# Batches 4 to 7 of the first product by seven products, behind all attention; PSUM as eight named banks

## The chip, the core and the metric

The kernel runs on one core of a Trainium2 chip. The metric is device microseconds of one execution. The kernel before takes 393.91 us (median of three runs, 393.77 to 394.09). The engines are named as in the profile: PE is the matrix engine (TensorE), PEld its weight loads, DVE the vector engine, ACT the scalar engine, POOL and SP the two engines that mostly issue transfers here. SBUF is the memory that the engines work from, PSUM the small one that PE writes its products to.

## The reference

Two layers are chained. The first is attention with 8 batches, 12 heads, 448 tokens and 64 numbers per head; the second is a feed-forward pair of products with a SiLU gate between them, 768 to 2048 to 768, over all 3584 tokens. Inputs to the kernel are cast to fp16 in SBUF's tiles.

```python
scores = scale * np.matmul(q, k.transpose(0, 1, 3, 2))
scores = scores - np.max(scores, axis=-1, keepdims=True)
attn = np.exp(scores)
attn = attn / (np.sum(attn, axis=-1, keepdims=True) + 1e-09)
attn_out = np.matmul(attn, v)
x = attn_out.transpose(0, 2, 1, 3).reshape(B * S, H * D)
h = x @ w_in
g = h * (1.0 / (1.0 + np.exp(-h)))
out = g @ w_out
```

## The kernel before

**Attention.** The twelve heads of a batch go in three groups of four; a group of one batch is a unit, and batch 0 is cut into two pieces of tokens, so that there are 27 units. POOL issues the loads of K (tile `rk`), Q (`rq`) and V. DVE turns K and Q (`turn_k`, `turn_q`, L302 and L312). PE makes a burst of scores (`scores`, `scores_rest`, L325): the four heads sit in four groups of 32 rows of the array and run side by side, one head to a bank of PSUM. ACT takes the exponential (`expo`, L362) of two heads at a time, 128 x 896 numbers, into a tile `E`. For most units DVE adds three `E` tiles into `T` (`add_e`, L373) for the sums of the softmax; PE makes the sums (`attend_sums`, L404, or `attend` with part 0, L388) and the two halves of the product with V (`attend`, L388; parts 1 and 2). DVE turns, inverts and turns back the sums (`inverse`, L447, L455, L461) and scales the product into `xT` (`norm`, L477).

**First product.** For batches 0 to 5, `ffn1` (L491) makes one bank of 128 features x 448 tokens in six products (chunks of 128 of the 768 inputs). ACT takes tanh of it into `th` (`tanh`, L502), DVE makes the gated value from `th` and the bank (`gate`, L536) and writes it to `G`, or for some tokens of batches 1 and 5 to `X`. `norm` halves x, so that (1 + tanh) * h is the wanted SiLU.

Batches 6 and 7 are done as a pair by Strassen's scheme in Winograd's form (`pair_product`, L625). The two batches and the two halves of the 768 inputs make a 2 x 2 matrix of blocks, the halves of the inputs and of the 2048 features another. Seven block products of three matrix products each replace eight. For that, DVE makes four sums of x (`combine_x`, L583, tiles `sx`) and four sums of w_in in two halves (`combine_w_in`, L601, tiles `tw`). For each of the eight values of f, the seven products come in the order 1, 6 and 7, 5, 2, 3, 4, and take four banks. Their readers are two copies on ACT (`pair_copy`, L650), five additions on DVE (`pair_add`, L656) and four SiLUs on ACT (`silu`, L663).

**Second product.** Tiles of 128 tokens go in pairs ("quads", fourteen of them). The first quad is a plain product (`plain`, L710); the others go by the same scheme, seven products of eight matrix products with 384 columns (`product`, L696). DVE makes four sums of `G` for each (`combine_g`, L686, tiles `S`) and the additions behind it (`take_6` and its like, L750), ACT two copies (L754, L757). SP stores the results; the last quads' stores are shared with ACT's queue.

**PSUM.** Eight banks: two tiles of two banks (tag `s`) for scores, four tiles of one bank (tag `m`) for everything else. The pair borrows one `s` tile.

**The order.** The order on every engine is fixed when the kernel is built. A class `Order` plays the work through with costs per operation. At each point it chooses for PE among the next burst of scores (not more often than `PACE`), the next attention product and the first of the queue `moe` whose inputs and banks are free; for ACT and DVE it chooses the ready operation with the lowest time plus `bias`. POOL's loads are in one fixed order, each waiting for its buffer. A whole `ffn1` group of six products, or eight for a quad, is one piece of work and isn't interrupted. Until the first `ffn1` group, PE's waits are filled with small products of zeros (L1459). A change of kind on PE, between products that use the whole array and the four-way ones of scores (by rows) or attention (by columns), costs the planner `SWITCH`.

Of the kernel before, what the change touches and what calls it, by code (L numbers as in the profile page):

```python
# [17 lines left out]
PE_OUT = 0.20  # L18
# [11 lines left out]
def act(n):  # L30
    return n * 0.00087 + 0.13


class Ring:


    def __init__(self, n):
        self.free = [0.0] * n

    def can(self, n, now):  # L40
        return len(self.free) >= n and heapq.nsmallest(n, self.free)[-1] <= now

    def when(self, n):
        return heapq.nsmallest(n, self.free)[-1] if len(self.free) >= n else None

    def take(self, n=1):
        for _ in range(n):
            heapq.heappop(self.free)

    def give(self, at):  # L50
        heapq.heappush(self.free, at)
# [25 lines left out]

class Order:


    def __init__(self, shy):
        self.now, self.shy = 0.0, shy
        self.free = {"PE": 1.0, "ACT": 2.1, "DVE": 1.2, "POOL": 1.2}
        self.wait = {"ACT": [], "DVE": []}
        self.pool = []
        self.dma_free = 0.0
        self.out = []
        self.mode = None
        self.busy = {e: 0.0 for e in self.free}
# [16 lines left out]
    def on_pe(self, op, mode):  # L106
# [3 lines left out]
        self.start(op)  # L110

# [54 lines left out]
def kernel(  # L166
# [36 lines left out]
    SHY = 0.5  # L203
    TWB, SXB = 4, 4
    PIECES = ((0, 7), (7, TPP))
    NE, NX3, NT_ = 9, 6, 2
# [29 lines left out]

    rawk, rawq, KT, QT, VT, E, T, acc, rdn_t, xT, g_t, ost_t = ({} for _ in range(12))
# [24 lines left out]
    def load_v(b, hg0, hg1, x):  # L262
        if b not in VT:
            VT[b] = sb.tile([128, NH, NCH, D], FP16, name=f"V_{b}", tag="V", bufs=2)
        hs = slice(HG * hg0, HG * hg1)
        first, count = X_TOK[form(b, hg0)][x]
        nc.gpsimd.dma_start(  # L267
            out=VT[b][32 * x : 32 * (x + 1), hs, 0:count, :],
# [46 lines left out]
    def score_banks(n, w, ys):  # L315
        for y in ys:
            pS_t[(n, w, y)] = ps.tile(
                [128, 2, 512], FP32, name=f"s_{n}_{w}_{y}", tag="s", bufs=2
            )

    def score(pS, n, c, e, h, x0, x1, p0):
# [4 lines left out]
            out=pS[p0 : p0 + 32 * (x1 - x0), h % 2, at : at + nq],  # L326
# [3 lines left out]
            stop=(e == 1),  # L330
        )
# [5 lines left out]
    def scores(n, w, ys):  # L337
        score_banks(n, w, ys)
        for c in range(per_burst(n) * w, per_burst(n) * (w + 1)):
            for e in range(2):  # L340
                for y in ys:
                    for h in (2 * y, 2 * y + 1):
                        score(pS_t[(n, w, y)], n, c, e, h, 0, rows_of(n, c) // 32, 0)


    def scores_rest(n):
        score_banks(n, 3, (0, 1))
        for e in range(2):
            for h in range(HG):
                pS = pS_t[(n, 3, h // 2)]  # L350
# [6 lines left out]
    def expo(n, w, y):  # L357
        kr = rows_of(n, w * per_burst(n))
        nk = 32 * (units[n][3] - units[n][2]) * per_burst(n)
        if (n, w) not in E:  # L360
            E[(n, w)] = sb.tile([128, HG, S], FP16, name=f"E_{n}_{w}", tag="E", bufs=NE)
        nc.scalar.activation(  # L362
            out=E[(n, w)][0:kr, 2 * y : 2 * y + 2, 0:nk],
            in_=pS_t[(n, w, y)][0:kr, :, 0:nk],
# [15 lines left out]
    def attend_mm(a, n, part, c, h, k0, k1, e, start, stop):  # L380
# [5 lines left out]
        else:  # L386
            w = VT[b][k0:k1, HG * hg + h, c, part - 1 :: 2]
# [5 lines left out]
            stop=stop,  # L393
        )

    def attend_sums(ns):
        a = ps.tile([128, 512], FP32, name=f"a_{ns[0]}_0", tag="m", bufs=4)
        for n in ns:
            acc[(n, 0)] = a
        for i, (w, e) in enumerate(  # L400
            ((half[0], T[ns[0]]), (half[1], T[ns[1]]), (both, E[(ns[0], 3)]))
        ):
            for h in range(HG):
# [5 lines left out]
                    stop=(i == 2),  # L409
                )  # L410

    def attend(ns, part):
# [4 lines left out]
        for n in ns:  # L417
            acc[(n, part)] = ps.tile([128, 512], FP32, name=f"a_{n}_{part}", tag="m", bufs=4)

# [22 lines left out]
    def inverse(ns, step, i=0):  # L442
        g0, g1 = units[ns[0]][2:]
        shape = [128, g1 - g0, 32]
        if step == 0:
            sT_t[ns[0]] = sb.tile(shape, FP32, name=f"sT_{ns[0]}", tag="sT", bufs=1)
# [11 lines left out]
        else:  # L458
            n = ns[i]
            rdn_t[n] = sb.tile(shape, FP32, name=f"rdn_{n}", tag="rdn", bufs=2)  # L460
            nc.vector.transpose(  # L461
                out=rdn_t[n], in_=inv_t[ns[0]][:, :, i : i + 1].to_broadcast(shape)
            )

    def x3(b, cc):
        if (b, cc // 3) not in xT:
            xT[(b, cc // 3)] = sb.tile(
                [128, 3, S], FP16, name=f"xT_{b}_{cc // 3}", tag="xT", bufs=NX3
            )
        return xT[(b, cc // 3)]  # L470

    def norm(n, part):
# [3 lines left out]
        x3(b, cc)  # L476
        nc.vector.scalar_tensor_tensor(  # L477
            out=x3(b, cc)[:, cc % 3, 32 * g0 : 32 * g1],
# [7 lines left out]
    h_t, th_t, o_t = {}, {}, {}  # L486

    def ffn1(b, f, t0, t1):
        h = ps.tile([128, 512], FP32, name=f"h_{b}_{f}_{t0}", tag="m", bufs=4)
        for cc in range(NDC):  # L490
            nc.tensor.matmul(  # L491
                out=h[:, 0 : t1 - t0],
                lhsT=w_in_t[:, cc, 128 * f : 128 * (f + 1)],
                rhs=x3(b, cc)[:, cc % 3, t0:t1],
                start=(cc == 0),
                stop=(cc == NDC - 1),
            )
        h_t[(b, f, t0)] = h

    def tanh(b, f, t0, t1):  # L500
        th = sb.tile([128, t1 - t0], FP16, name=f"th_{b}_{f}_{t0}", tag="th", bufs=3)
        nc.scalar.activation(out=th, in_=h_t[(b, f, t0)][:, 0 : t1 - t0], func=AF.Tanh)  # L502
        th_t[(b, f, t0)] = th

# [6 lines left out]
    X = const.tile([128, NFF, 128], FP16, name="X")  # L511
# [18 lines left out]
    def gate(b, f, t0, t1):  # L530
        r = b % 2
        cut = 6 * 128 - S if b % 4 == 1 else S
        for lo, hi, dst, at in ((0, cut, G, S * r), (cut, S, X, -cut)):
            lo, hi = max(lo, t0), min(hi, t1)
# [1017 lines left out]
```

## Time and profile before

| | |
|---|---|
| median of three runs | 393.91 us |
| profiled execution, span from first to last instruction | 393.0 us (the profile gives no other time of that execution) |
| PE busy | 386.6 us, 98% |
| DVE busy | 296.2 us, 75% |
| ACT busy | 238.7 us, 61% |
| exponentials (L362) | 172, 150.0 us of ACT |
| granted clock of PE | 0.998 |

The page gives busy time by engine and by line, the chain of work that ended last, who waited for whom, and the instructions in order of time. A busy share near 100% on PE says that some product is always under way, not that it is done at full rate; for that the distance between the starts of neighbouring products is read.

### The profile page before, as it was taken

What the parts mean: (1) busy time and instruction counts of PE and PEld (TensorE: products, weight loads), DVE (VectorE), ACT (ScalarE), POOL (GpSimd) and SP (SyncE); (2) the same over time, 40 slices, a digit from 0 to 9 for tenths busy, and PEclk for the clock granted to TensorE, in tenths of its full rate; (3) what the DMA queues carried; (4) which work ended last, traced back from release to release, by engine and by line L of the source; (5) the groups of instructions that cost most, each with busy time, mean ns of one, the idle gap of its engine ahead of it and who ended that gap; (6) DMA issues with size and microseconds to landing.
All of it is one profiled execution on the core that took longest, in us unless ns stands there. A gap on an engine that the chain in (4) does not pass through costs nothing.

```text
span 393.0 us, 9255 instructions
## 1 busy us (share of the span) xinstructions
PE 386.6 (98%) x3679; PEld 199.7 (51%) x3679; DVE 296.2 (75%) x610; ACT 238.7 (61%) x365; POOL 83.7 (21%) x153
## 2 busy tenths in 40 slices
PE   8999999999999999999999999999999999999996
PEld 7667774444444434454444444444444555555663
DVE  2476676999988696895968967876879897777652
ACT  4988885696855869626778258575693218772000
POOL 6632455406006060600063116000000000000000
PEclk9999999999999999999999999999999999999999
DMA  7999999919047573753183567202000140001443
GB/s 112 205 210 210 161 166 179 182 37 141 2 82 115 109 103 39 121 99 86 25 116 48 102 125 115 38 2 61 21 3 2 46 100 17 2 1 37 97 98 93
DMA packets 35579, 34.43 MB, mean 88 GB/s; under 512 B 11600, under 2 KB 34000, under 8 KB 35536
## 3 DMA queue, kind: packets, MB, share of 16 engines
q0 software_dynamic: 24784, 22.82, 39.2%
q1 hardware_dynamic: 9984, 10.24, 10.2%
q10 hardware_dynamic: 768, 0.79, 0.8%
q8 instruction: 29, 0.48, 0.5%
q14 instruction: 14, 0.11, 0.1%
HBM read 45.61 MB, written 11.01 MB: 144 GB/s over the span
## 4 chain that ended last, share of the span: by engine, by line
PE 94%; DMA 2%; DVE 1%; ACT 1%; issue 0%; POOL 0%; SPq 0%; ACTq 0%; DVEq 0%; POOLq 0%
PE p L696 29%; PE h L491 29%; PE s L325 12%; PE a L388 10%; PE f L625 8%; PE o L710 3%; PE a L404 2%; DMA rk<-in_k_dram 2%; DMA out_dram<-ost 1%; PE z L1459 1%; DVE tw L601 0%; ACT E L362 0%; DVE ost L750 0%; SPq L745 0%; DVE KT L302 0%
## 5 line engine op out<-in xcount | busy, mean ns | idle before, releaser
L362 ACT ACTIVATE E<-s 128x896 f16<-128x896 f32 (+1 forms) x172 | 150.0, 915 | 44.9 <-PE s L325 43.6
L491 PE MATMUL h<-xT,w_in_t 128*128 128x448 f16 (+1 forms) x672 | 118.2, 326 | 0.0
L491 PEld LDWEIGHTS <-w_in_t 128*128 128x128 f16 x672 | 61.5, 98 | 54.4 <-issue 17.7
L502 ACT ACTIVATE th<-h 128x448 f16<-128x448 f32 (+1 forms) x112 | 54.3, 494 | 33.6 <-PE h L491 24.9
L536 DVE SCALAR_TENSOR_TENSOR G<-th,h 128x448 f16<-128x448 f16 (+2 forms) x112 | 55.4, 508 | 16.5 <-ACT th L502 14.7
L267 POOL DMA_DIRECT2D V<-in_v_dram x88 | 48.6, 568 | 50.2 <-PE a L388 35.7
L325 PE MATMUL s<-rq,KT 32*128 32x448 f16 (+4 forms) x864 | 56.7, 340 | 0.8 <-ACT E L362 0.4
L696 PEld LDWEIGHTS <-G 128*128 128x128 f16 x384 | 36.3, 98 | 28.5 <-issue 4.8
L696 PEld LDWEIGHTS <-S 128*128 128x128 f16 x312 | 29.5, 98 | 23.8 <-issue 3.4
L388 PE MATMUL a<-E,V 128*32 128x448 f16 (+3 forms) x864 | 39.9, 334 | 0.0
L696 PE MATMUL p<-w_out_t,S 128*128 128x384 f16 x208 | 38.1, 326 | 0.5 <-DVE xT L477 0.5
L696 PE MATMUL p<-D,G 128*128 128x384 f16 x208 | 38.1, 326 | 0.0
L252 POOL DMA_DIRECT2D rq<-in_q_dram x27 | 15.1, 560 | 104.7 <-PE s L325 88.7
L750 DVE TENSOR_TENSOR ost<-p,u 128x384 f32<-128x384 f32 x39 | 21.6, 555 | 19.4 <-PE p L696 15.5
L477 DVE SCALAR_TENSOR_TENSOR xT<-a,rdn 128x448 f16<-128x448 f32 (+1 forms) x54 | 28.6, 565 | 7.0 <-PE a L388 6.2
L325 PEld LDWEIGHTS <-KT 32*128 32x128 f16 (+2 forms) x864 | 17.5, 98 | 28.9 <-issue 26.0
L696 PE MATMUL p<-w_out_t,G 128*128 128x384 f16 x176 | 31.9, 326 | 0.0
L373 DVE TENSOR_TENSOR T<-T,E 128x1792 f16<-128x1792 f16 x20 | 21.7, 1087 | 10.2 <-ACT E L362 10.2
L388 PEld LDWEIGHTS <-V 128*32 128x32 f16 (+2 forms) x864 | 17.8, 95 | 20.8 <-issue 13.5
L373 DVE TENSOR_TENSOR T<-E,E 128x1792 f16<-128x1792 f16 x20 | 21.6, 1082 | 5.5 <-ACT E L362 5.5
L757 ACT COPY ost<-p 128x384 f32<-128x384 f32 x13 | 6.2, 480 | 32.0 <-PE p L696 21.1
L302 DVE STREAM_TRANSPOSE KT<-rk 128x256 f32<-128x256 f32 (+3 forms) x48 | 16.7, 386 | 6.8 <-DMA rk<-in_k_dram 6.8
(70 smaller groups left out, 344.5 us busy)
## 6 DMA issues: line engine op xcount, KB each, us to landing
out_dram<-ost SPq DMA_DIRECT2D x208, 48.0 KB, 1.6
rk<-in_k_dram POOLq DMA_DIRECT2D x24, 224.0 KB, 5.0
rq<-in_q_dram POOLq DMA_DIRECT2D x21, 224.0 KB, 5.4
w_in_t<-in_moe_w_in_dram POOLq DMA_DIRECT2D x6, 512.0 KB, 11.4
w_out_t<-in_moe_w_out_dram POOLq DMA_DIRECT2D x4, 768.0 KB, 13.6
V<-in_v_dram POOLq DMA_DIRECT2D x43, 64.0 KB, 4.0
V<-in_v_dram POOLq DMA_DIRECT2D x40, 48.0 KB, 3.9
out_dram<-ost ACTq DMA_DIRECT2D x16, 48.0 KB, 1.8
```

The source lines that it names most:

```text
L267: nc.gpsimd.dma_start(out=VT[b][32 * x : 32 * (x + 1), hs, 0:count, :], in_=v[b, hs].rearrange("h (i g) d -> i h g d", g=TPP)[:, :, first ...
L325: nc.tensor.matmul(out=pS[p0 : p0 + 32 * (x1 - x0), h % 2, at : at + nq], lhsT=KT[(b, hg)][32 * h : 32 * (h + 1), c, x0:x1, :, e], rhs=QT[ ...
L362: nc.scalar.activation(out=E[(n, w)][0:kr, 2 * y : 2 * y + 2, 0:nk], in_=pS_t[(n, w, y)][0:kr, :, 0:nk], func=AF.Exp, scale=attn_scale,)
L373: nc.vector.tensor_tensor(out=T[n], in0=T[n] if step else E[(n, 0)], in1=E[(n, step + 1)], op=ALU.add,)
L388: nc.tensor.matmul(out=a[32 * h : 32 * (h + 1), 0:nq], lhsT=w, rhs=e[k0:k1, h, at : at + nq], start=start, stop=stop,)
L477: nc.vector.scalar_tensor_tensor(out=x3(b, cc)[:, cc % 3, 32 * g0 : 32 * g1], in0=acc[(n, part)][:, 0:nq], scalar=0.5, in1=rdn_t[n].rearra ...
L491: nc.tensor.matmul(out=h[:, 0 : t1 - t0], lhsT=w_in_t[:, cc, 128 * f : 128 * (f + 1)], rhs=x3(b, cc)[:, cc % 3, t0:t1], start=(cc == 0), s ...
L502: nc.scalar.activation(out=th, in_=h_t[(b, f, t0)][:, 0 : t1 - t0], func=AF.Tanh)
L536: nc.vector.scalar_tensor_tensor(out=dst[:, f, at + lo : at + hi], in0=th_t[(b, f, t0)][:, lo - t0 : hi - t0], scalar=1.0, in1=h_t[(b, f, ...
L625: nc.tensor.matmul(out=pp_t[(f, PBANK[m])], lhsT=w[:, c, :], rhs=a[:, c, :], start=(c == 0 and m in (1, 6, 5, 7)), stop=(c == 2), skip_gro ...
L696: nc.tensor.matmul(out=pr_t[(qd, BANK[m])][:, 0:OH], lhsT=w[:, f, :], rhs=W_[m][:, f, :], start=(f == 0 and BANK[m] == m), stop=(f == HF - 1),
L750: nc.vector.tensor_tensor(out=out, in0=a, in1=b, op=op)
```

## The change

The diff replaces much of the planner's bookkeeping and many of its constants. What it does to the work:

- Batches 4 and 5 become a pair as well; only batches 0 to 3 go through `ffn1`. The two pairs are queued in the order 4 and 5, then 6 and 7, and `deps()` of a pair's products returns nothing ready while any score burst is left, so that they stand behind all attention. `xT` gets 8 tiles instead of 6; batch 7's x lies in `rk` tiles. The first SiLU, in front of which ACT loads a table, stands behind the last exponential and the last gate of batch 3 (`exp_end`).
- PSUM is one tile `P` of eight banks. In batch 0 scores take three pairs of banks and the other work two banks. After that a burst of scores takes banks 0, 1 and 2 and one bank from the ring of the other five; `expo` then reads three heads in one instruction (128 x 1344) and the fourth in another (128 x 448). When the last burst is read, all eight banks are in the ring.
- `ffn1`, a quad's product and a pair's product are issued one matrix product at a time (`in_steps`), so that a burst of scores or an attention product can come in between.
- tanh goes straight into `G` and `gate` works there in place; `X` is only used for batch 5. Batch 0's pieces take two features to a bank. `inverse` turns both units' inverses back in one instruction. Sums for quads below 7 are made in one instruction each instead of two.
- V is loaded to tiles of one head group, four of them, instead of two tiles of a batch; batch 0's V is put into `G`. `E` has 11 tiles instead of 9. The pair's `v` goes to a V tile, `q` to a fixed buffer `R`.

```diff
-    PACE = 2.6
+    PACE = 2.8
...
-    EAGER = 1
-    HALVES = 6
-    NEAR, LATE = 0.15, -2.0
+    EAGER = 3
+    HALVES = 1
+    PAIRS = (B - 4, B - 2)
+    LAST = {B - 4: range(DFF // 256), B - 2: range(DFF // 256)}
...
-    NE, NX3, NT_ = 9, 6, 2
+    NE, NX3, NT_, NV = 11, 8, 2, 4
...
+    P = ps.tile([128, 8, 512], FP32, name="P")
+    R = const.tile([128, 2, S // 32, 32], FP32, name="R")
...
+    def in_steps(self, op, each, steps):
+
+        assert not self.steps
+        self.steps = [
+            Op("PE", each, fn, tail=op.tail) for fn in steps
+        ]
+        self.steps[-1].then = lambda at: self.whole(op, at)
+        self.next_step()
+
+    def whole(self, op, at):
+        op.done = at
+        if op.then:
+            op.then(at)
+
+    def next_step(self):
+        self.on_pe(self.steps.pop(0), "full")
...
-    def expo(n, w, y):
-        kr = rows_of(n, w * per_burst(n))
+    def expo(n, w, h0, h1):
+        kr, bank = rows_of(n, w * per_burst(n)), pS_t[(n, w)][h0]
...
-            out=E[(n, w)][0:kr, 2 * y : 2 * y + 2, 0:nk],
-            in_=pS_t[(n, w, y)][0:kr, :, 0:nk],
+            out=E[(n, w)][0:kr, h0:h1, 0:nk],
+            in_=P[0:kr, bank : bank + h1 - h0, 0:nk],
...
-    s_ring, m_ring, e_ring = Ring(2), Ring(4), Ring(NE)
-    rk_ring, rq_ring, v_ring = Ring(NRK), Ring(NRQ), Ring(2)
+    s_ring, m_ring, e_ring = Ring(0, (0, 1, 2)), Ring(0, (6, 7)), Ring(NE)
+    rk_ring, rq_ring, v_ring = Ring(NRK), Ring(NRQ), Ring(NV)
...
     def run_qk():
         ns, c, ys = qk_seq.pop(0)
...
-        s_ring.take(len(ys))
+        if b == 0:
+            tiles = dict(zip(ys, s_ring.take(len(ys))))
+            parts = [(2 * y, 2 * y + 2, (2 * j, 2 * j + 1)) for y, j in tiles.items()]
+        else:
+            lone = m_ring.take()[0]
+            parts = [(0, 3, (0, 1, 2)), (3, 4, (lone,))]
+            for x in range(3):
+                s_free[x] = None
...
+    def give_banks(at, banks):
+        if qk_seq and units[qk_seq[0][0][0]][0] == 0:
+            s_ring.give(at, banks[0] // 2)
+            return
+        for x in banks:
+            if x > 2:
+                m_ring.give(at, x)
+            else:
+                s_free[x] = at
...
             def deps():
+                if qk_seq:
+                    return [None]
                 made = [xs[0, c] for c in (range(3, NDC) if m == 2 else range(3))]
...
+            n = HF if qd < WHOLE else HF // 2
+            for f0 in range(0, HF, n):
...
-        if b == PB:
-            return
-        if b > PB:
-            queue_pair()
-            for qd in range(1, NT * B // 4):
-                if max(batches(qd)) >= PB:
-                    queue_quad(qd)
+        if b >= PAIRS[0]:
+            if b - 1 in PAIRS:
+                queue_pair(b - 1)
+                for qd in range(1, NT * B // 4):
+                    if max(batches(qd)) in (b - 1, b):
+                        queue_quad(qd)
             return
```

More of the change, by code (lines that the diff above doesn't have):

```diff
@@ L1174, in run @@
                 elif m == 6:
-                    read(6, "DVE", take_6, [op, took[1]], m_ring.give)
+                    read(6, "DVE", take_6, [op, took[1]], m_ring.giver(bank[6]))
                 elif m == 2:
-                    read(2, "ACT", take_2, [op], both())
+                    read(2, "ACT", take_2, [op], both(1))
                 elif m == 7:
@@ L1247, in moe_ready @@
             if banks:
-                free = m_ring.when(1)
+                free = m_ring.when(banks + held)
                 if free is None:
@@ L1313, in run_qk @@
         od.on_pe(op, "rest rows" if rest else "rows")
-        for y in ys:
+        for h0, h1, banks in parts:
             made = od.add(
```

763 lines of the change are left out of this document (446 added, 317 removed).

## The prediction

> **What bounds the kernel now.** I read the page's busy times first, then the chain of work that ended last, then the distances between products in that chain, to see whether PE is only busy or also at its rate.
>
> ```profile
> span 393.0 us, 9255 instructions
> PE 386.6 (98%) x3679; PEld 199.7 (51%) x3679; DVE 296.2 (75%) x610; ACT 238.7 (61%) x365; POOL 83.7 (21%) x153
> PEclk9999999999999999999999999999999999999999
> PE 94%; DMA 2%; DVE 1%; ACT 1%; issue 0%; POOL 0%; SPq 0%; ACTq 0%; DVEq 0%; POOLq 0%
> ```
>
> The chain is PE for 94% of the span. From the chain in order of time (start, length, what):
>
> ```profile
> 284.50 2.38 PE h L491 x12
> 286.88 0.51 PE s L325 x8
> 287.38 2.38 PE h L491 x12
> 307.93 1.82 DVE tw L601 x2
> 309.75 0.55 DVE xT L477
> 310.34 2.77 PE p L696 x16
> 321.48 30.08 PE f L625 x159
> 353.99 32.61 PE p L696 x200
> 386.62 0.57 DVE ost L750
> ```
>
> A product with 448 columns takes 30.08 / 159 = 0.189 us, one with 384 columns 32.61 / 200 = 0.163 us. Twelve products and one burst of scores take 287.38 - 284.50 = 2.88 us, so a burst with its two changes of kind costs 2.88 - 12 x 0.189 = 0.61 us. Such steps follow each other without gaps from the first `ffn1` product, at 30.23 us (its row is below), to 386.62; the only visible stall is the one behind the rows of 307.93 and 309.75, where PE waited 0.53 us for DVE. So three things set the time: the start up to 30.2, the sum of PE's work, and an end of 393.0 - 386.62 = 6.4 us. The page gives no other time for this execution; the median of the runs, 393.91, is 0.9 above its span, and I carry that 0.9 along.
>
> **The products.** By count in the two built orders: `ffn1` loses 192 products of 448 columns (batches 4 and 5, 16 features, 6 each), the second pair adds 168 (8 x 7 x 3). 24 x 0.189 = 4.54 us less. Scores, attention, quads and plain products are the same in number and shape. From the first `ffn1` product on PE changes kind 182 times before and 183 times after, so cutting groups into single products costs nothing there. I take -4.5; ends -4.8 and -4.3 (one or two changes of kind).
>
> **The start.**
>
> ```profile
> 6.22 0.60 PE L325 MATMUL s<-rq,KT 32*128 32x224 f16 x16
> 13.99 0.40 PE L1459 MATMUL z<-zeros 128*128 128x128 f16 x4
> 14.32 0.57 PE L325 MATMUL s<-rq,KT 32*128 32x224 f16 x8
> 18.99 0.60 PE L325 MATMUL s<-rq,KT 32*96 32x224 f16 x8
> 19.52 0.57 PE L388 MATMUL a<-E,V 128*32 128x224 f16 x16
> 20.02 0.60 PE L325 MATMUL s<-rq,KT 32*96 32x224 f16 x8
> 30.23 0.75 PE L491 MATMUL h<-xT,w_in_t 128*128 128x224 f16 x6
> 6.83 3.33 ACT L362 ACTIVATE E<-s 128x896 f16<-128x896 f32 x4 [4.80 <-PE s L325]
> 11.55 12.03 ACT L362 ACTIVATE E<-s 128x896 f16<-128x896 f32 x13 [0.30 <-PE s L325]
> 29.45 0.91 ACT L362 ACTIVATE E<-s 96x896 f16<-96x896 f32 x1 [0.56 <-PE s L325]
> ```
>
> ACT's 24 exponentials of batch 0 run from 6.83 to 30.36, 23.5 us, where back to back (12.03 / 13 = 0.925) they need 22.2. In the second half PE sets the pace: score and attention alternate at 20.02 - 18.99 = 1.03 us. The changed order issues scores in pairs, 0.53 us for sixteen (6.22 to the next row at 6.75), and has three double banks, not two; then ACT paces. Gain between 0 and 23.5 - 22.2 = 1.3; I take 0.9, since the first waits, for K and Q, stay. The 57 extra products of zeros, 57 x (14.32 - 13.99) / 4 = 4.7 us, stand in PE's waits: PE's own sum from 6.2 to the first `ffn1` product becomes some 22 us (scores 11 x 0.53 + 2 x 0.5, attention 11 x 0.5 + 2 x 0.9, zeros 97 x 0.083) against the 24.0 it took, so a loss is excluded.
>
> **The attention stage.** Exponentials: the shape 128 x 1344 isn't in the trace.
>
> ```profile
> L362 ACT ACTIVATE E<-s 128x896 f16<-128x896 f32 x156 | 136.0, 915 | 43.3 <-PE s L325 42.4
> L502 ACT ACTIVATE th<-h 128x448 f16<-128x448 f32 x80 | 43.7, 546 | 31.0 <-PE h L491 23.3 <-issue 5.1 <-ACT th L502 2.3
> L536 DVE SCALAR_TENSOR_TENSOR G<-th,h 128x448 f16<-128x448 f16 x48 | 28.7, 614 | 7.0 <-ACT th L502 6.1
> L477 DVE SCALAR_TENSOR_TENSOR xT<-a,rdn 128x448 f16<-128x448 f32 x42 | 24.1, 615 | 3.9 <-PE a L388 3.7
> L373 DVE TENSOR_TENSOR T<-E,E 128x1792 f16<-128x1792 f16 x20 | 21.6, 1082 | 5.5 <-ACT E L362 5.5
> 143.47 1.16 DVE L477 SCALAR_TENSOR_TENSOR xT<-a,rdn 128x448 f16<-128x448 f32 x2 [0.28 <-PE a L388]
> 75.00:100.00 25.00, 25.00 (x237) 10.50 (x230) 23.73 (x51) 19.66 (x30) 8.69 (x16) 1.00 0.60 88
> 94.01:118.26 24.25, 24.25 (x241) 11.18 (x244) 21.54 (x49) 15.55 (x23) 1.04 (x2) 1.00 0.37 65
> 118.26:141.84 23.58, 23.58 (x232) 10.38 (x236) 18.58 (x34) 15.97 (x23) 9.84 (x18) 1.00 0.64 109
> ```
>
> By the line through 0.546 for 448 and 0.915 for 896 numbers it takes 1.284; with the fourth head's 0.546 that is 1.83 a burst, as two of 0.915 before: nothing. Ends: 0.37 less (one instruction's fixed part) and 0.18 more a burst. All attention now stands in front of both pairs: 74 bursts after batch 0 fall in about 210 us of PE work instead of some 265, and ACT and DVE have to keep up. I added up the changed orders with these rows (busy time over count for DVE, since neighbours overlap). ACT: 173 us in the 206 of PE work of twelve blocks of six bursts; the tightest are the first, 15.9 of 16.0, and the eighth, 15.8 of 16.1. DVE: 170.9 of 179.7 us between the ten products for sums, 95%; the first three stages 61.6 of 62.6, the last 23.5 of 23.0, since the sums of w_in and x for the pair lie there. Before, such stages were at 79 to 89% (the last two rows; columns are span, PE, PEld, DVE, ACT).
>
> The row nearest to 95% is that of 75 to 100 us: DVE 23.73 of 25.00, PE 25.00, no stall. Held strictly to that share, the four stages above it would stretch by 61.6 / 0.95 - 62.6 = 2.2 and 23.5 / 0.95 - 23.0 = 1.7, together 3.9; at the 89% of the second-last row all nine would take 192.0, 12.3 more. I take 1.5, between nothing and 3.9, because part of what fills DVE (turns of K and Q, sums of w_out) is wanted only later. Ends: 0 and 12.3.
>
> [...]
>
> **The pairs.** The first pair keeps the five additions, two copies and four SiLUs for each f; of eight rows of each kind:
>
> ```profile
> L656 DVE TENSOR_TENSOR u<-f,u 128x448 f32<-128x448 f32 x8 | 5.0, 625 | 0.8
> L663 ACT ACTIVATE G<-p 128x448 f16<-128x448 f32 x8 | 4.6, 578 | 1.6 <-DVE p L656 1.6
> L650 ACT COPY q<-f 128x448 f32<-128x448 f32 x8 | 4.3, 534 | 11.4 <-PE f L625 11.4
> 321.50:351.56 30.06, 30.06 (x161) 15.56 (x160) 23.49 (x39) 23.09 (x43) 0.00 (x0) 1.00 0.06 16
> ```
>
> Of 168 x 0.189 = 31.8 us of PE, DVE has 40 x 0.625 = 25.0 plus 4.6 of late sums, ACT 8 x (4 x 0.578 + 2 x 0.534) = 27.0 plus 16 split SiLUs at 0.18, 29.9: 93 and 94%, where the pair before (last row) had 78 and 77% and ran dense. Two sets of four banks, now all eight being free, take up single delays. I take 0 and keep 3 as the upper end. The second pair has 25.4 of DVE: 0.
>
> **Edits at nothing.**
>
> ```profile
> rk<-in_k_dram POOLq DMA_DIRECT2D x24, 224.0 KB, 5.0
> rq<-in_q_dram POOLq DMA_DIRECT2D x21, 224.0 KB, 5.4
> ```
>
> The last four quads are in the same pattern as before, so the end stays 6.4. Loads and stores are the same in number, POOL's in the same order. V now waits for one of four tiles of a head group, with K's and Q's loads queued behind it on POOL; but four groups ahead are some 40 us (a stage of 20 us, 179.7 / 9, holds two), and loads land after 5.0 to 5.4 us: cover enough. The table load goes with the SiLUs behind the last exponential; quads cover it. Merged sums save fixed parts of DVE and are in the sums above.
>
> **Sum.** 393.9 - 4.5 - 0.9 + 1.5 = 390.0.
>
> **Rivals.** (1) DVE becomes the bound in the attention stage: the kernel is slower. Place: the first three stages and the last. It needs DVE below 170.9 / (179.7 + 5.4) = 92.3% of its time with work; for it speaks that no grouped stage before exceeds 89%, against it the window at 95% without a stall. At 91% the stages take 187.8, 8.1 more: 393.9 - 5.4 + 8.1 = 396.6.
>
> (2) The first pair is bound by its readers. At 85% use DVE's 29.6 take 34.8, 3.0 more than PE: 390.0 + 3.0 = 393.0, no gain worth measuring. For it: copies and SiLUs of several f interleave in the order. Against it: eight banks.
>
> (3) The fixed score banks starve ACT. A burst can start only when the three-head exponential is done.
>
> ```profile
> 129.03 0.57 PE L325 MATMUL s<-rq,KT 32*128 32x448 f16 x8
> 129.64 1.73 ACT L362 ACTIVATE E<-s 128x896 f16<-128x896 f32 x2 [1.49 <-PE s L325]
> ```
>
> From burst to exponential pass 0.61 us, and PE may first finish a product of 0.19; ACT has the fourth head's 0.546 meanwhile, so up to 0.25 a burst stays open unless a tanh fills it. Over 74 bursts that fits in ACT's 33 us of slack; in the two tight blocks it would cost 12 x 0.25 = 3.0: 393.0. Against it: these very blocks have a tanh beside nearly every burst. [...]
>
> **Chances.** Forecast 0.55 (its own range 387.5 to 392.5: the start's and products' ends, stalls 0 to 3.9); (1) 0.20; (2) 0.13; (3) 0.12. 386.8 to 396.6 leaves out half of (1) and little below. A difference of 0.2%, 0.8 us, is about what can be told from none. Faster: nearly all of the forecast and half of (2) and (3), 0.67; same 0.07; slower 0.26.
>
> **What would show it.** Right: the first `ffn1` product near 29; products in the first pair 0.189 apart; PE about 382 busy, no row of PE waiting for DVE over a microsecond in all. Wrong: waits of PE on DVE after 60 us (1), on the pair's copies or additions (2), or ACT waiting for score bursts while PE waits for banks (3).

## The result

The changed kernel takes 391.24 us (median of four runs, 390.20 to 391.49) where the kernel before took 394.0 beside it; the ratio is 0.9918 with an interval of 0.9904 to 0.9933. It is faster, by 2.8 us, and 1.2 us slower than the 390.0 forecast. Of one kernel below, the one with halves alone, eight of twelve runs took 402 to 406 us at a mean granted clock of 0.96 to 0.97, which stays open, and its figures are those of the other four.

The page of the changed kernel: span, busy times, granted clock, and the chain's shares.

```profile
span 389.4 us, 9280 instructions
PE 380.4 (98%) x3712; PEld 198.2 (51%) x3712; DVE 294.9 (76%) x543; ACT 242.9 (62%) x381; POOL 83.7 (21%) x153
PEclk9999999999999999999999999999999999999999
PE 93%; DMA 4%; DVE 1%; issue 1%; POOL 0%; SPq 0%; DVEq 0%; POOLq 0%
```

PE bounds it as before, but the chain's shares of DMA and "issue" have grown, and what was added lies in the start. The end of the chain, in order of time (start, length, what):

```profile
240.80 0.53 PE P L380 x16
241.33 7.91 PE P L772 x48
249.24 0.68 PE P L457 x12
...
258.33 31.78 PE P L692 x168
290.12 27.30 PE P L772 x168
317.42 30.64 PE P L692 x162
...
350.50 32.51 PE P L772 x200
...
383.03 0.57 DVE ost L824
```

The last burst of scores starts at 240.80, the last sums at 249.24, and from 258.33 the pairs and quads run without a gap: 31.78 / 168 = 0.189 us a product, as before. From 34 us on no row of PE names an engine that it waits for. The end is 389.4 - 383.0 = 6.4 us. So nothing was lost after the start. The first `ffn1` product, though, is late, and the rows of PE just before it say why (start, length, work, then the idle time ahead of it and what ended that):

```profile
6.09 0.96 PE L380 MATMUL P<-rq,KT 32*128 32x224 f16 x24
...
19.85 0.22 PE L1644 MATMUL P<-zeros 128*128 128x128 f16 x1 [0.48 <-DVE xT L549]
...
21.20 0.57 PE L442 MATMUL P<-E,cols 128*32 128x224 f16 x15 [0.94 <-issue]
...
27.40 0.35 PE L442 MATMUL P<-E,G 96*32 96x224 f16 x5 [1.68 <-issue]
...
31.68 0.44 PE L1644 MATMUL P<-zeros 128*128 128x128 f16 x5 [0.48 <-DVE xT L549]
31.96 1.22 PE L561 MATMUL P<-xT,w_in_t 128*128 128x224 f16 x11
```

Its start is at 31.96 us, against 30.23 before. One trace is a rough measure of that: six of the kernels below have the same 576 products in front of it, in the same order, and in the seven traces it starts between 30.26 and 33.25. What the start costs is therefore taken from the medians below. PE stops twice in the middle of an attention product, for 0.94 and 1.68 us, with nothing to wait for that the profile shows. The kernel before had one such stop, in the same view:

```profile
28.60 0.28 PE L388 MATMUL a<-E,cols 96*32 96x224 f16 x3 [0.23 <-issue]
```

Counted from the start of the program, the two stops of the changed kernel stand behind 348 and 476 products, and the one before behind 476 too. The distance is 128 products, 256 instructions with their weight loads. Between 15 and 30 us the loads move 210 GB/s, and two packets of instructions go through among them (queue, packets, MB, share):

```profile
DMA packets 1757, 3.15 MB, mean 210 GB/s; under 512 B 125, under 2 KB 517, under 8 KB 1755
...
q8 instruction: 2, 0.03, 0.8%
```

By the trace they start at 18.98 and 25.02 us, 2.2 and 2.4 us before PE goes on at 21.20 and 27.40. That gave the first theory: PE's code comes in blocks of 128 products, and a block that has to queue among the loads of the start takes about 6 us (27.40 - 21.20 = 6.2 from stop to stop).

One more correction. In every later run of the kernel before, a run's time lies 1.7 to 1.8 us above its span. The profiled execution of before, span 393.0, was therefore one of about 394.8 us, 0.9 above the median; the prediction took this 0.9 for time outside the span. The traces' difference of 3.6 us and the medians' of 2.8 differ by it.

### The profile page after: what moved, and what is told of

It is laid out like the page before. It is cut to its first block, busy times and chain, and to the rows that moved or that the text cites. A ratio compares the mean times of both kernels' runs of the same rounds, so it can differ in the third digit from the quotient of the medians.

```text
span 389.4 us, 9280 instructions
## 1 busy us (share of the span) xinstructions
PE 380.4 (98%) x3712; PEld 198.2 (51%) x3712; DVE 294.9 (76%) x543; ACT 242.9 (62%) x381; POOL 83.7 (21%) x153
## 4 chain that ended last, share of the span: by engine, by line
PE 93%; DMA 4%; DVE 1%; issue 1%; POOL 0%; SPq 0%; DVEq 0%; POOLq 0%
PE P L772 31%; PE P L561 20%; PE P L692 16%; PE P L442 10%; PE P L380 10%; PE P L784 3%; DMA rq<-in_q_dram 2%; PE P L457 2%; DMA rk<-in_k_dram 1%; PE P L1644 1%; DMA out_dram<-ost 0%; DVE xT L549 0%; DVE ost L824 0%; DVE R L498 0%; DVE KT L362 0%
## 5 line engine op out<-in xcount | busy, mean ns | idle before, releaser
L416 ACT ACTIVATE E<-P 128x448 f16<-128x448 f32 (+4 forms) x172 | 151.8, 920 | 52.1 <-PE P L380 51.4
L561 PE MATMUL P<-xT,w_in_t 128*128 128x448 f16 (+1 forms) x480 | 81.5, 316 | 0.0
L380 PE MATMUL P<-rq,KT 32*128 32x448 f16 (+4 forms) x864 | 50.4, 340 | 0.3 <-ACT E L416 0.3
L602 DVE SCALAR_TENSOR_TENSOR G<-G,P 128x448 f16<-128x448 f16 x64 | 38.3, 608 | 14.7 <-ACT G L577 14.3
L772 PE MATMUL P<-D,G 128*128 128x384 f16 x208 | 39.1, 327 | 0.0
L772 PE MATMUL P<-w_out_t,S 128*128 128x384 f16 x208 | 38.9, 326 | 0.0
L577 ACT ACTIVATE G<-P 128x448 f16<-128x448 f32 x64 | 34.3, 549 | 6.9 <-PE P L561 6.6
L772 PE MATMUL P<-w_out_t,G 128*128 128x384 f16 x192 | 35.2, 327 | 0.0
L442 PE MATMUL P<-E,V 128*32 128x448 f16 (+2 forms) x672 | 34.2, 355 | 0.0
L692 PE MATMUL P<-sx,tw 128*128 128x448 f16 x144 | 29.9, 352 | 0.0
L380 PEld LDWEIGHTS <-KT 32*128 32x128 f16 (+2 forms) x864 | 14.1, 98 | 24.7 <-issue 22.3
```

Source lines behind the costliest of these rows:

```text
L380: nc.tensor.matmul(out=P[p0 : p0 + 32 * (x1 - x0), pS[h], at : at + nq], lhsT=KT[(b, hg)][32 * h : 32 * (h + 1), c, x0:x1, :, e], rhs=QT[n ...
L416: nc.scalar.activation(out=E[(n, w)][0:kr, h0:h1, 0:nk], in_=P[0:kr, bank : bank + h1 - h0, 0:nk], func=AF.Exp, scale=attn_scale,)
L442: nc.tensor.matmul(out=a[32 * h : 32 * (h + 1), 0:nq], lhsT=w, rhs=e[k0:k1, h, at : at + nq], start=start, stop=stop, skip_group_check=True,)
L561: nc.tensor.matmul(out=h_t[(b, f, t0)][:, 0 : t1 - t0], lhsT=w_in_t[:, cc, 128 * f : 128 * (f + 1)], rhs=xc(b, cc)[:, t0:t1], start=(cc == 0),
L577: nc.scalar.activation(out=g, in_=h, func=AF.Tanh)
L602: nc.vector.scalar_tensor_tensor(out=g, in0=g, scalar=1.0, in1=h, op0=ALU.add, op1=ALU.mult)
```

## The experiments

All changes are made to the changed kernel. Runs of before beside them had medians of 394.2 to 394.4.

**No zeros behind the first 47.**

```diff
-        if warm["on"] and od.free["PE"] <= od.now and wait > 0.06 and od.now > 0.9:
+        if "first" in warm and warm["on"] and od.free["PE"] <= od.now and wait > 0.06 and od.now > 0.9:
```

> The changed kernel without the products of zeros behind the first 47 (97 of 144 are left out; they write columns that nobody reads). In the changed kernel the first ffn1 product starts at 31.96 us, 1.73 later than before. Theory code: PE had no work to issue for 0.94 us at product 348 and for 1.68 us at product 476, a distance of 128 products, and the kernel before had its one such gap, 0.23 us, at the same product 476; a block of 128 products is fetched among the loads and takes some 6.2 us in this stage, so the 57 extra products of zeros cost about 57 x 6.2 / 128 = 2.8 us. Then here, with 400 products ahead of the first ffn1 product, gaps of this kind add up to less than 0.5 us, the first ffn1 product starts at 29.0 to 29.5, and the time is 388.3 to 389.0. Theory bank: zeros share bank 7 with attention, and the waits of 0.48 and 0.48 us of PE on DVE in front of zeros made the loss; then they go and about 1 us is won, 390.2, and the gaps stay. Rival: zeros keep PE's clock up; without them the granted clock falls in the first 60 us and the time is 392 or more.

Measured: 389.19 us (388.49 to 389.66), ratio to before 0.9868 [0.9855, 0.9880]: 2.05 us less than the changed kernel and the fastest kernel of this study. It is 0.2 above the range of the code theory and 1.0 below the bank theory's time. No gap without work is left, as the code theory said. The clock did fall, for a shorter time than the rival needs. The windows of PE (span, busy, products, granted clock, DMA share, GB/s):

```profile
8.00:10.00 2.00, 1.10 (x33) 1.00 1.24 182
10.00:12.00 2.00, 1.53 (x26) 0.75 1.45 193
12.00:14.00 2.00, 1.23 (x16) 0.50 1.44 202
16.00:18.00 2.00, 2.00 (x48) 0.54 1.10 207
18.00:20.00 2.00, 1.78 (x64) 1.00 1.13 212
```

By these windows the clock was halved from about 11 to 18 us. The zeros cost more than the seven microseconds or so at half clock that they prevent. (The planner also puts some `ffn1` products earlier here, so the start of the first of them, 24.53, can't be compared.)

**The start's banks and halves as before.**

```diff
-    HALVES = 1
+    HALVES = 6
...
-    s_ring, m_ring, e_ring = Ring(0, (0, 1, 2)), Ring(0, (6, 7)), Ring(NE)
+    s_ring, m_ring, e_ring = Ring(0, (0, 1)), Ring(0, (4, 5, 6)), Ring(NE)
...
-                warm["on"] = False
+                if warm["on"]:
+                    warm["on"] = False
+                    m_ring.give(od.now, 7)
```

> The changed kernel with the start's banks and halves as before: in batch 0 scores take two pairs of banks and are issued by halves (HALVES 6), the other work takes three banks, and bank 7 holds zeros alone until the first ffn1 product. The order then has 87 zeros and 521 products ahead of the first ffn1 product, as before. Both theories of the start (code blocks, shared bank): first ffn1 product at 30.2 us as before, gaps without work at most 0.3 us, time 391.2 - 1.7 = 389.5. If instead the loss at the start comes from something else that changed (V in G, inverses in one instruction, V's tiles), it stays at 391.2.

Measured: 389.74 us (389.54 to 389.78), ratio 0.9883 [0.9869, 0.9898], 1.50 less than the changed kernel, as both theories of the start expected within 0.3. Rows of PE from its trace:

```profile
28.05 0.40 PE L380 MATMUL P<-rq,KT 32*96 32x224 f16 x3 [0.88 <-issue]
29.90 1.32 PE L561 MATMUL P<-xT,w_in_t 128*128 128x224 f16 x12
```

The first `ffn1` product is back at 29.90. One stop of 0.88 is left, where 0.3 at most was expected, again behind 476 products. V in `G`, the merged inverses and V's tiles, which stay changed here, are not the cause.

**Wide zeros: half as many, of 256 columns.**

```diff
-        for _ in range(n):
+        for _ in range((n + 1) // 2):
             nc.tensor.matmul(
-                out=P[:, 7, 384:512],
+                out=P[:, 7, 256:512].rearrange("p (a c) -> p a c", a=2),
                 lhsT=zeros,
-                rhs=zeros,
+                rhs=zeros.rearrange("p (a c) -> p a c", a=1).to_broadcast([128, 2, 128]),
```

> The changed kernel with zeros of 256 columns, half as many (87 in place of 144, since odd numbers are rounded up), in the same bank and at the same places: PE spends as long on zeros, but its stream has 57 products fewer, 521 ahead of the first ffn1 product. Theory code: the gaps at products 348 and 476 shrink from 2.62 us to 0.5 or less, first ffn1 product between 29.5 and 30.5, time 389.0 to 389.8. Theory bank: nothing changes, 31.5 to 32.5 and 391 to 391.6.

Measured: 390.37 us (389.81 to 390.99), ratio 0.9899 [0.9887, 0.9912]. Two rows of PE from its trace in order of time:

```profile
28.84 0.37 PE L442 MATMUL P<-E,G 96*32 96x224 f16 x5 [0.74 <-issue]
31.59 1.22 PE L561 MATMUL P<-xT,w_in_t 128*128 128x224 f16 x11
```

The stop behind 348 products is gone and the one behind 476 is down from 1.68 to 0.74. Alone that shows little: two kernels below, whose products up to there are the changed kernel's (24 products more, and the first with four score banks), have no stop behind 348 either. What shows that the stops hang on the count of instructions is their place. In twelve of the fourteen traces PE stops in this way, always behind 222, 348 or 476 products, whatever product comes next. In the traces of before and of the changed kernel it goes on 2.2 to 2.4 us after a packet of the instruction queue has started (26.34 us before, 18.98 and 25.02 in the changed kernel). That queue moved 29 packets for the 3679 products of before and 29 for the 3712 of the changed kernel, about one to 128 products.

Together the stops are 0.94 + 1.68 - 0.74 = 1.88 us shorter here than in the changed kernel's trace. Against that the zeros, rounded up, keep PE 1.6 us longer (15.1 us busy for 13.5), which leaves 0.3; the first `ffn1` product is 31.96 - 31.59 = 0.37 earlier, and the median 0.9 lower, with intervals that overlap (0.9887 to 0.9912 and 0.9904 to 0.9933). Both waits of zeros on DVE (0.48 each) remain, so the shared bank is a second cause beside the stops. The time of the code theory is missed; that this is because the edit costs PE time of its own is argued from these sums, not shown.

**Halves alone.**

```diff
-    HALVES = 1
+    HALVES = 6
```

> The changed kernel with HALVES 6 alone: batch 0's scores by halves, but its banks as changed (three pairs for scores, two banks for the rest, zeros in bank 7, which the others share). 90 zeros, 524 products ahead of the first ffn1 product. Theory code: as the kernel before, gaps of 0.3 us or less, first ffn1 product near 30.3, time 389.6. Theory bank: zeros still wait for DVE, first ffn1 product near 31.5 to 32, time 391.

Neither: 394.0 to 395.8 us, ratio 1.0014 [1.0001, 1.0026]. The start did as the code theory says, with the first `ffn1` product at 30.41 and a stop of 0.66 (0.3 or less was expected). The loss stands elsewhere, in the order at the end of the attention stage (rows of DVE and PE in order of time):

```profile
245.66 0.62 DVE L549 SCALAR_TENSOR_TENSOR xT<-P,R 128x448 f16<-128x448 f32 x1 [0.21 <-issue]
246.20 2.69 DVE L674 TENSOR_TENSOR tw<-w_in_t 128x1536 f16<-128x1536 f16 x3
...
249.41 1.68 DVE L549 SCALAR_TENSOR_TENSOR xT<-P,R 128x448 f16<-128x448 f32 x3
251.00 0.55 DVE L824 TENSOR_TENSOR ost<-P,u 128x384 f32<-128x384 f32 x1
...
251.60 1.74 PE L772 MATMUL P<-D,G 128*128 128x384 f16 x5 [3.22 <-DVE ost L824]
```

Three sums of w_in for the pair (2.69 us) got ahead of the last three `xT` on DVE, so PSUM's banks were not emptied and PE stood for 3.22 us. The changed kernel also has three sums of w_in in front of its last `xT`, four of them in one go, but no row of PE waits there. Why the planned order came out so here is open.

**Zeros off, with the start's banks and halves as before.** The edits of the first two experiments together.

> The start's banks and halves as before (as in e2_start_before) and no zeros behind the first 47 (as in e1_no_zeros). e1 won 2.05 us and e2 1.50 against the changed kernel. If zeros cost by their blocks of code and by waits for the shared bank alone, the bank of its own in e2 leaves only the blocks, and e7 lies near e1: 388.5 to 389.2. If what zeros cost is the place in PE's order (work that the planner puts behind them), it gains the same 2 us again: 387.7. If the granted clock, which fell to 0.91 in the first 36 us of e1, costs more with PE idle for longer: 390 or more.

Measured: 401.40 us (400.47 to 406.28), ratio 1.0202 [1.0165, 1.0240]: the third case, far beyond its number. Windows of PE in its trace, columns as in the first experiment:

```profile
10.00:12.00 2.00, 2.00 (x34) 0.61 1.44 188
...
32.00:34.00 2.00, 2.00 (x44) 0.50 1.13 208
```

Here PE ran at half clock from about 10.5 to 34 us and the first `ffn1` product came at 37.03. 3.22 us more were lost at the same place as with halves alone. Score bursts by halves leave PE enough small work to look busy (2.00 of 2.00) and yet the clock did not come back, where in the first experiment it came back at about 18 us. What separates the two is open.

**Zeros in the first 16 us only.**

```diff
-        if warm["on"] and od.free["PE"] <= od.now and wait > 0.06 and od.now > 0.9:
+        if (od.now < 16.0 or "first" in warm) and warm["on"] and od.free["PE"] <= od.now and wait > 0.06 and od.now > 0.9:
```

> The changed kernel with zeros only in the first 16 us of the planned order: 115 of the 144 stay, the 29 behind are left out, those among attention products that share bank 7 and whose code blocks arrive late. Two effects were seen apart: with no zeros at all the start got shorter, but the granted clock was 0.50 from about 11 to 17 us (e1_no_zeros) and from 11 to 34 us (e7_e2_no_zeros, 401 us). Theory: the early zeros hold the clock, the late ones only cost. Then the clock stays 1.00 all through, the first ffn1 product starts by 28 us, and the time is at or below that of e1_no_zeros: 387.7 to 389.2. Rival early: it is the early zeros that cost, by the code blocks they use up: 390.3 to 391.3. Rival clock: the clock falls as soon as zeros stop: 391 or more.

Measured: 390.76 us (389.44 to 391.26), ratio 0.9903 [0.9887, 0.9918], not to be told from the changed kernel; it falls in the range of the rival that puts the cost on the early zeros. A row of PE from its trace:

```profile
21.37 0.37 PE L442 MATMUL P<-E,cols 96*32 96x224 f16 x7 [1.72 <-issue]
```

This is again the stop behind 348 products, and it is 1.72 us long, not 0.94: by the code theory the early zeros, all still there, use up the blocks, and the stop comes in front of work that is needed. The second stop behind 476 and the waits of zeros on DVE are gone. The clock did not stay at 1.00, as the theory had it; soon after the long stop it was halved for some 3.4 us (a window of PE, columns as in the first experiment; the windows before and behind it have 0.87 and 0.78):

```profile
24.00:26.00 2.00, 2.00 (x44) 0.50 1.13 213
```

The order that follows, the same as without any zeros, gives most of what was won back behind the start: when products worth 30 us are done (by the sum described under whole groups) this kernel is 1.8 us ahead of the changed one, at 310 us still 0.45.

**24 products more.** Each p1 of the first pair is computed twice.

```diff
-                op = Op("PE", 3 * len(ms) * mm(S), None, tail=PE_OUT)
+                twice = 2 if pb == PAIRS[0] and m == 1 else 1
+                op = Op("PE", 3 * twice * len(ms) * mm(S), None, tail=PE_OUT)
...
-                    [lambda x=x, c=c: pair_product(pb, f, x, c) for x in ms for c in range(3)],
+                    [lambda x=x, c=c: pair_product(pb, f, x, c) for x in ms for _ in range(twice) for c in range(3)],
```

> The changed kernel with the three products of p1 computed twice for each of the first pair's 8 features (24 more products of 448 columns; the second time overwrites the first, the output stays). Theory PE: from the first ffn1 product on the kernel is as long as PE's products, and the gain of the change behind the start is the 24 products it saves; putting 24 back costs 24 x 0.189 = 4.5 us: 395.6 to 396.0. Rival readers: the first pair is held by the copies, additions and SiLUs (93 and 94% by their rows in the prediction), so that products there are partly free: 391.5 to 394.

Measured: 395.54 us (394.20 to 396.22), 4.3 more than the changed kernel (4.6 by the ratios to before, 1.0034 and 0.9918). The chain's row of the first pair:

```profile
256.64 35.19 PE P L692 x186
```

35.19 / 186 = 0.189: the pair is as long as its products, and its readers have room. So the saving of 24 products is what this change gains; the start takes part of it back.

**All first additions twice, then ten of them** (in the second run `n % 4 < 2` stands for `True`).

```diff
-        nc.vector.tensor_tensor(
+        for _ in range(2 if step == 0 and True else 1):
+            nc.vector.tensor_tensor(
...
-                od.add(Op("DVE", 1.08, lambda n=n: add_e(n, 0), exp_op[n][0:4], ADD_B))
+                od.add(Op("DVE", 2.16 if True else 1.08, lambda n=n: add_e(n, 0), exp_op[n][0:4], ADD_B))
```

> The changed kernel with each of the 20 first additions of exponentials (T from two E) done twice: 20 x 1.08 = 21.6 us more for DVE, all in the attention stage, same output. Theory rows: DVE's rows are its time; with 170.9 of 179.7 us it had 8.8 to spare, so the stage becomes at least 192.5 - 179.7 = 12.8 longer: 404 or more. [...]

> As e6_double_additions, but 10 of the 20 first additions are done twice, 10.8 us more for DVE in the attention stage (the copies q into R wait for the last xT of batch 7, which read R; output unchanged). e6 gave 18.5 us for 21.6. Theory slack: DVE had 179.7 - 170.9 = 8.8 to spare by its rows, so about 2 us are lost here, 392.5 to 394.5. Rival no slack: the stage was already as long as DVE, and all 10.8 show: 400 or more. Rival much slack: 391 to 392.

Measured: 409.74 us (407.54 to 409.95) with twenty, 18.5 more than the changed kernel; 393.49 (392.01 to 394.23) with ten, 2.2 more. The 2.2 are in the range of the theory of slack, but the trace shows only a small part of them to be the additions': DVE holds up PE for 0.6 us in the whole stage. The first `ffn1` product came at 33.25, 1.3 later than in the changed kernel's trace, and that is no price of the additions, the first of which starts at 51.27. PE's clock was halved there (a window of PE):

```profile
30.00:32.00 2.00, 2.00 (x38) 0.50 1.11 211
```

So DVE had more to spare than the theory says, and what of the 2.2 is the additions' isn't settled. Twenty don't fit, as the theory of rows said (404 or more). The loss with twenty lies mostly in one place. Windows of the engines (span; busy time and count of PE, PEld, DVE, ACT, POOL; clock, DMA share, GB/s):

```profile
120.00:130.00 10.00, 7.18 (x94) 2.78 (x78) 9.77 (x15) 6.81 (x8) 6.54 (x12) 0.81 0.81 107
140.00:150.00 10.00, 6.88 (x37) 2.79 (x40) 7.07 (x10) 1.60 (x2) 0.00 (x0) 0.50 0.08 21
```

Once DVE is late (9.77 of 10.00), bursts stand without filling work between them, PE waits 1.4 us for exponentials at 125.39 and at 127.39 and 3.1 us for DVE at 144.51, and meanwhile the clock halves as well.

**Whole groups in place of single products.**

```diff
     def in_steps(self, op, each, steps):
+        op.emit = lambda: [fn() for fn in steps]
+        self.on_pe(op, "full")
+        return
```

> The changed kernel with ffn1, quads and pair products issued as whole groups again, not one product at a time (in_steps undone; q into R waits for the last xT of batch 7). Prediction's view, edits at nothing: the same sum of products and about the same number of changes of kind, 390.7 to 391.7. Rival steps: in the dense attention stage bursts and attention have to come in between single products, or ACT and DVE are fed too late by up to 1.1 us a time: 393 to 397.

Measured: 401.18 us (400.58 to 401.74), ratio 1.0172 [1.0158, 1.0186], 9.9 more than the changed kernel: the rival's direction, beyond its range, and not by its mechanism, for the dense stage is no slower. As a common measure of work the products other than zeros are added up by their columns, 2.4 columns to the ns, a round unit for the sum (448 in 0.189 us, the price above, are 2.37), a quarter for the four-way ones (16 more of 224 columns add 0.96 - 0.57 = 0.39 us, 0.024 each). The work from 30 to 210 us of this sum took 196.2 us here and 197.6 in the changed kernel. The loss is at the end of the stage. First the chain of this kernel in order of time, then a window of its engines:

```profile
246.93 0.58 PE P L382 x8
247.50 3.00 PE P L444 x63
250.50 0.56 PE P L382 x8
251.07 1.29 ACT E L418
252.35 0.04 issue
...
257.60 1.29 ACT E L418
258.88 0.04 issue
258.93 0.97 PE P L382 x13
```

```profile
250.00:260.00 10.00, 4.42 (x61) 1.32 (x54) 6.47 (x9) 6.95 (x9) 0.00 (x0) 0.73 0.02 6
```

`ffn1` and the quads ran out before the bursts did, and the pairs must wait for the last burst. The bursts left over run alone, each waiting for the three-head exponential of the one before (1.29 us), and PE's clock drops to 0.73 meanwhile. The planner's constants (`PACE` and its like) are those of the changed kernel; whether others would spare the whole groups this end is open. The copy `q` waits for the last `xT` of batch 7 here, as it does in the kernel with ten additions, which has no such end.

**Four score banks, two exponentials of two heads.** In the first run the copy `q` overwrote `R` before the last three `xT` of batch 7 had read it, so that batch 7's values are others; the second run puts the copy behind them. The amount of work is the same in both. Besides the lines shown, `score_banks` asks for four fixed banks, and no bank is kept back for a burst.

```diff
-            lone = m_ring.take()[0]
-            parts = [(0, 3, (0, 1, 2)), (3, 4, (lone,))]
-            for x in range(3):
+            parts = [(0, 2, (0, 1)), (2, 4, (2, 3))]
+            for x in range(4):
                 s_free[x] = None
...
-            if x > 2:
+            if x > 3:
                 m_ring.give(at, x)
```

> The changed kernel with PSUM's split undone behind batch 0: a burst takes four fixed banks, two exponentials of two heads each read them (0.915 us each by the rows before), the other work has four banks. Theory PE: scores were never what PE waited for, so nothing changes: 390.7 to 391.7. Rival banks: the fourth bank that comes and goes is needed by the steps of ffn1 and attention between bursts; with four banks PE waits, 392.5 to 395. Rival fixed banks: the three-head exponential held the next burst back; then this is faster, 389.5 to 390.5.

> As e10_four_score_banks, in which the copy q overwrote R before the last three xT of batch 7 had read it, so that its output is not that of the reference; here q waits for them. e10 took 403.95, as dense as the changed kernel up to the last two groups of attention (useful work of 210 us reached at 251.1 against 252.0), and lost 11 us behind that. Theory end: four banks of scores and four of the rest are enough while ffn1 and quads stand between the bursts, and the loss is that the last bursts come too late and have nothing beside them; it stays: 400 to 404, with PE waiting for exponentials and additions between 240 and 280 us. Rival: the loss was the early copy of the pair, then 391 to 393.

Measured: 403.95 (402.66 to 404.88) and 404.53 us (404.38 to 404.93); the copy was not the cause. It is the theory of the end, as rows of PE of the second run show:

```profile
254.12 0.37 PE L380 MATMUL P<-rq,KT 32*128 32x448 f16 x2 [0.86 <-ACT E L416]
254.93 0.57 PE L380 MATMUL P<-rq,KT 32*128 32x448 f16 x6 [0.44 <-ACT E L416]
...
261.97 0.96 PE L380 MATMUL P<-rq,KT 32*64 32x448 f16 x12 [0.22 <-ACT E L416]
```

By the same sum as above, the work from 30 to 210 us took 198.3 us against 197.6, so the split of PSUM is worth under a microsecond in the dense stage; from 210 to 240 it took 42.9 against 30.4. Here too the planner's constants were left as they were.

## Why the prediction was right, and where it was wrong

**The products, -4.5: right.** Putting 24 back cost 4.3 by the medians, 4.6 by the ratios, and the rows give 0.189 each.

**The start, -0.9: wrong, and the step that failed is "so a loss is excluded".** The start as before is 1.50 us faster than the changed one (389.74 against 391.24; 1.4 by the ratios), so the term is +1.5, 2.4 away. PE's own sum held: from 6.09 to 31.96 are 25.9 us, and less the stops and waits shown (0.94, 1.68 and twice 0.48) they are 22.3, where "some 22" was forecast. It left out what would stop PE. The 57 more zeros, costed at nothing because they "stand in PE's waits", had two prices that the sum didn't have. One is PE's code: from stop to stop 128 products took 27.40 - 21.20 = 6.2 us, and in the other traces with two or three stops it is 5.9 to 6.3 us for 126 or 128, so by the code theory zeros in a wait use up a block that the next burst then lacks. The stops 128 products apart (each with its weight load) and the two packets of 0.03 MB in all between 15 and 30 us agree with that. That PE stops for its code is read from the packets, 2.2 to 2.4 us behind whose start it goes on in the traces of before and of the changed kernel; that the packets come so late because of the loads is argued, for no run thinned the loads out. The other is the bank: there are two banks for attention, not three, and the zeros write into one of them, so DVE's `xT` waits for zeros and zeros wait for `xT` (a row of DVE in the changed kernel):

```profile
28.23 0.39 DVE L549 SCALAR_TENSOR_TENSOR xT<-P,R 128x224 f16<-128x224 f32 x1 [2.11 <-PE P L1644]
```

Most of these 2.11 us are the stop of 1.68 in the attention product before it, which ended at 27.75; the zeros behind that product end at 28.19 and add some 0.4. Leaving all these zeros out won 2.05 us, with the price of the half clock already taken off. How the 1.5 to 2 us of the medians divide between blocks, bank and the order that follows isn't settled: no run took away one of them and left the others as they were.

**DVE in the attention stage, +1.5: no stall came, and the step that failed is 170.9 us taken for DVE's time.** The stage was forecast as 179.7 us between the ten products for sums with 170.9 of DVE, 95%. The trace of the changed kernel, same columns as above:

```profile
70.89:249.17 178.28, 178.28 (x1858) 75.33 (x1854) 155.05 (x257) 136.25 (x189) 51.35 (x94) 1.00 0.53 85
```

The stage is as long as forecast and has the 257 instructions, but they cover 155.05 us, 87%: busy times of groups were added up, in which only neighbours of one group overlap and not those of different groups, and the sum was then held against busy shares of windows, in which that overlap is gone already. No row of PE waits for DVE in the stage, and the stall term is 0. The durations of the same 257 add up to 171.5 us, 16.4 more than they cover: 64 ns a row lie beside other rows. That DVE can bind is so all the same: ten additions more made PE wait 0.6 us, twenty cost 18.5.

**The pairs, the end, edits at nothing.** 0.189 a product in both pairs and 6.4 us at the end, as said. Issuing single products costs nothing, as said, but it is not indifferent: without it, and with the constants left alone, the kernel takes 9.9 us longer. The new exponential was put at 1.284 by a line through two rows. Groups of the changed kernel, shapes kept apart:

```profile
L416 ACT ACTIVATE E<-P 128x1344 f16<-128x1344 f32 x72 | 93.0, 1292 | 41.9 <-PE P L380 41.2
L416 ACT ACTIVATE E<-P 128x448 f16<-128x448 f32 x72 | 39.6, 550 | 0.0
```

It takes 1.292 and, with 0.550 for the fourth head, 1.84 a burst, as two of 0.915 before.

**The sum.** 393.9 - 4.5 + 1.5 + 0 = 390.9, with 391.24 measured. The forecast's two errors, -2.4 and +1.5, partly cancelled, so that 390.0 came as near as it did is partly luck: with the DVE term right and the start as forecast it would have said 388.5. Its own range of 387.5 to 392.5 doesn't follow from the ends that it names; they give 393.9 - 4.8 - 1.3 = 387.8 and 393.9 - 4.3 + 3.9 = 393.5. Of its signs, 0.189 us in the first pair and no long wait for DVE came true, and PE was busy for 380.4 us, not 382; the first `ffn1` product near 29 did not. Rivals (1) and (2) did not occur. Of rival (3) the changed kernel shows nothing, but its mechanism is what the whole groups show when no other work is left beside the bursts.

## What to carry to other kernels

Filling work is not free merely because it stands in the waits of the bound engine: leaving 97 products of zeros out won 2.05 us here. Such products use instructions, and PE stopped behind 348 and 476 products for 0.94 and 1.68 us; and they use a bank that somebody else wants, with two waits of 0.48 us. When all work of one kind is put in front of another, look first at the point where the filling work could run out before the paced work does; here that point is worth 10 to 13 us, and three of the twelve kernels (whole groups, and both with four score banks) lost their time at it. Busy time from windows and sums of durations are two measures (155.05 and 171.5 us for the same 257 instructions of DVE); hold a sum only against a sum.

## What had not been expected of the hardware

PE stopped in the middle of a product group, always behind 222, 348 or 476 products, while the DMA engines moved 210 GB/s, up to 1.7 us a time; behind 34 us, where products are longer (220 in the 20 us from 45 to 65), no such stop was seen. The granted clock fell to 0.50 without any long wait: in the run without zeros PE was busy for 1.10 to 1.43 of each 2 us between 4 and 10 us, with single waits of at most 0.9 us, and got half clock from about 11 to 18 us. Worked out from the windows of PE, half clock lasted some 3.4 us with zeros in the first 16 us only, 6.8 without zeros and 23.9 without zeros and with the start's banks and halves as before. In the last of these PE's rows follow each other without a gap from 17 us on, and still the clock returned only at 34.
